# Mamba2 SSD and SwiGLU feed-forward on one core: the order of the steps from the 291st on, and two sums moved from GpSimd to VectorE

## The chip, the cores and the metric

One core of one Trainium2 chip runs the whole kernel in one launch. The metric is the device time of an execution in microseconds (us). The engines are TensorE (PE in the profile; its weight loads are PEld), VectorE (DVE), ScalarE (ACT), GpSimd (POOL) and SyncE (SP), which here issues nearly all the DMAs. Each engine runs its own list of instructions in order, and waits on semaphores for what the others give it.

## The reference

A state-space recurrence over 4 batches and 8 heads is followed by an RMS norm and a SwiGLU feed-forward. In the core of it (shapes: x is 4 x 8 x 768 x 32, B and C are 4 x 8 x 768 x 16, the chunk c is 32 long):

```python
L = np.exp(cum[:, :, :, None] - cum[:, :, None, :]) * causal
CB = np.einsum('bhin,bhjn->bhij', Cc, Bc)
y_intra = np.einsum('bhij,bhjd->bhid', CB * L, xc)
y_inter = np.einsum('bhin,bhnd->bhid', Cc, state) * np.exp(cum)[:, :, :, None]
y[:, :, sl] = y_intra + y_inter
state = decay_full * state + np.einsum('bhjn,bhjd->bhnd', Bc, xc * decay_from_j)
...
x = y.transpose(0, 2, 1, 3).reshape(3072, 256)
xn = x / np.sqrt(np.mean(x * x, axis=-1, keepdims=True) + 1e-06) * rms_g
g = xn @ w_gate                       # 256 -> 1536
out = (g / (1 + np.exp(-g)) * (xn @ w_val)) @ w_out      # 1536 -> 256
```

The weights come in float64, of which the kernel makes float32 itself; the rest is float32, and so is the output of 3072 x 256.

## The kernel before

The 3072 tokens go in six blocks of 512 (numbered 0 to 5). For each block the recurrence is computed in chunks of 128 rows for two pairs of batches, and then the feed-forward; the recurrence of one block runs between the feed-forward products of the one before it, so that TensorE always has something to do.

The products of gate and val of a block are made with seven products in place of eight on 2 x 2 pieces of the operands (steps `P.k.j`, product k of 1 to 7 for column group j of 0 to 5, line 977). They are gathered in two PSUM tiles, named gate and val in the profile; ScalarE copies one (`take`, name `p`, L983), VectorE adds the other (`C.c.j`, name `c`, L989), ScalarE applies silu (L208), and VectorE or GpSimd multiplies (`hid` or `hidp`, L1002), which gives the hidden activations `hid`.

The output projection is made with 20 products (`O.k`, each in two halves h from block 1 on, L1108) whose left factors are hidden pieces or sums of them and whose right factors are pieces of w_out or sums of those. The 16 sums of left factors are listed in `SUMS`; the step `u.n` makes sum n on VectorE and `up.n` makes it on GpSimd (both L1076). Number 7 is a42 = a42 + a43 and number 12 is a21 = a21 - a23, each over 128 x 4 x 128 elements, in place. The right factors (`two` and `twop`, name `two`, L1054) are summed once. The products' totals (`w.n`) are added into the tile `ob` by VectorE (L1139) or copied by ScalarE (L1135), and `put` sends it out (L1144).

In the recurrence, `T` and `g` (L599) make the transposed operands and the products C·B on TensorE, `L` and `L1` (L632) multiply them with the decays on VectorE, reading the PSUM banks of g; `A` (L678), `S` (L686 and L688) carry the states; `y` (L734) is the product that gives the outputs, into the banks that g leaves. `sq` squares y, `ms` (L846) sums the squares on TensorE, `rs` takes the roots on ScalarE and `rb` sends them through DRAM (`roots<-r` L859, then `sq<-roots` L864) so that all partitions have them; `xn` (L873) is the normed input, of which `tx` and `txp` (L954) make the sums that the seven products need. `spread` (DMA, `L<-rowd`, L500), `sub` and `ex` prepare the decays of a later block: an exponential on ScalarE, and a masking of the result on GpSimd (L493). ScalarE has one function table for exponentials and logarithms and one for silu; a step that needs the other one changes it first (L200, L202).

The weights come in 18 pieces. `fetch.k` issues the load of piece k (L184, name `wr`, six buffers), `pow.k` makes its exponents in two passes on ScalarE (name `e`), `man.k` its mantissas on VectorE (name `m`, L224), and `wt.k` joins them (L230). Pieces 12 to 17 are w_out.

What sets the order of all of it is one text of 1725 steps in the kernel, `order`. A step is written block:kind.numbers (with a slash and a number where a place in PSUM is named). The loop below it takes the steps one after the other and issues their instructions, so that the instructions of each engine stand in the order of the text. Some kinds serve the next block or the one after it, whichever block stands in front of the colon.

```python
for step in order.split():
    step, _, slots = step.partition("/")
    blk, _, step = step.partition(":")
    ...
    kind, *numbers = step.split(".")
    ...
        kinds[kind](int(blk), *numbers)
```

Of the kernel before, what the change touches and what calls it, by code (L numbers as in the profile page):

```python
# [20 lines left out]
def kernel(  # L21
# [35 lines left out]
    P = 128  # L57
# [6 lines left out]
    T = NB * S  # L64
# [1212 lines left out]
    def of_chunk(n, fn):  # L1277
# [57 lines left out]
        0:cwp.5.2 1:S.0 1:S.1 0:take.1.5 0:C.11.5 0:P.3.4 0:sq.3 0:man.12 0:cw.0.2 0:P.6.5 0:P.5.5  # L1335
        0:yt.3 0:silug.11.5 0:wt.12 0:hidgp.12.3 3:bc.0 0:C.12.4 0:sq2.2.1.3 0:sq2.2.0.0 0:fetch.17
        0:ms.1 0:take.6.5 0:P.7.5 0:sq2.2.1.2 0:sub.11 0:hidg.21.4 0:silug.22.4 0:hidgp.22.4
        0:sq2.2.0.3 0:sq2.2.1.1 0:fetch.14 0:rs.1 0:rb.1 0:cw.0.1 0:hidg.11.5 0:man.13 0:cwp.5.3
        0:ydone.2 0:man.15 0:take.7.5 0:C.22.5 0:pow.13 0:wt.13 0:o.0/2 0:o.1 0:P.4.5 0:silug.22.5
# [6 lines left out]
        1:silu.11.0 1:P.6.1 0:ex.11 1:P.5.0 0:O.0 0:hidg.12.5 1:two.8 0:O.17 1:P.2.1 0:O.6 0:tx.1.2
        1:two.11 0:cw.1.2 1:two.9 1:take.6.1 1:P.7.1 1:take.7.1 1:P.7.0 0:tx.1.3 1:C.11.1 0:w.5
        0:w.6 1:P.5.1 0:sq2.2.0.1 1:x.1 1:bc.0 0:spread.8 0:u.9 1:T.0.1 1:two.5 1:twop.7 0:O.3 0:w.4
        0:w.10 0:w.1 0:hidgp.22.5 0:up.4 0:u.5 0:up.6 0:cwp.1.3 0:ydone.3 1:silu.11.1 1:take.7.0
        0:hidg.12.4 1:P.4.1 1:silu.21.1 1:hid.21.1 1:cw.2.1 1:C.22.0 1:P.4.0 0:u.7 0:up.8 0:O.9  # L1350
        0:u.10 0:O.18 0:w.8 0:w.12 1:C.22.1 0:w.7 1:hid.11.0 1:P.1.2 0:O.8 0:ex.9 1:P.3.0 1:C.12.0
        0:O.13 1:T.1.1 1:silu.21.0 0:w.11 1:hid.21.0 1:take.1.2 1:Tt.0.1 1:Tt.1.0 1:P.3.1 1:P.6.2
        1:P.2.2 1:two.10 0:u.11 0:u.12 1:hid.11.1 1:twop.4 0:O.7 1:take.6.2 1:P.7.2 0:w.13 0:w.20
        1:C.11.2 0:O.12 0:u.14 0:sq2.2.0.2 0:w.9 1:T.1.0 1:P.1.3 0:O.11 0:w.22 1:sub.3 0:up.13
        0:O.14 0:u.15 0:w.18 1:silu.22.0 1:take.7.2 1:P.4.2 0:O.19 1:silu.12.0 1:hid.12.0
        1:hidp.22.0 1:take.1.3 1:P.6.3 1:ex.3 1:C.12.1 0:w.15 0:w.24 0:O.1 0:O.10 0:w.14 0:w.16
        1:T.0.0 0:w.19 0:w.21 0:w.23 0:w.25 0:put.2 1:sq2.1.0 0:put.0 1:P.2.3 1:P.5.2 1:C.22.2
        1:dT.1 1:spread.1 1:sq2.1.2 1:twop.6 1:cwp.2.3 0:O.5 0:w.17 1:silu.21.2 1:hid.21.2
        1:silu.12.1 1:hidp.12.1 1:take.6.3 1:P.7.3 1:sq2.0.3 0:put.3 1:Tt.0.0 1:silu.22.1
        1:hidp.22.1 1:silu.11.2 1:Tt.1.1 1:g 1:silu.22.2 1:hidp.22.2 1:take.7.3 1:P.4.3 1:silu.21.3  # L1360
        1:C.11.3 0:sub.10 1:silu.11.3 0:sub.8 0:ex.8 1:scale2.0 1:hid.21.3 1:P.3.2 1:C.12.2 1:sub.0
        1:hid.11.3 1:Td.1 1:P.1.4 1:take.1.4 0:ex.10 1:P.5.3 1:C.22.3 1:P.2.4 1:silu.12.2
        1:hidp.12.2 1:P.6.4 1:take.6.4 1:Td.0 1:C.11.4 1:hid.11.2 1:L 1:P.3.3 1:C.12.3 1:P.1.5
        1:take.1.5 2:dT.1 0:put.1 2:dT.0 1:sq2.0.2 1:P.7.4 1:take.7.4 1:P.5.4 1:C.22.4 1:silu.12.3
        1:P.6.5 1:P.2.5 1:L1.2 1:hid.12.3 1:C.11.5 1:P.4.4 1:silu.22.3 1:silu.22.4 1:hidp.22.4
        1:take.6.5 1:silu.21.4 1:silu.11.4 1:hid.21.4 1:hid.22.3 1:silu.11.5 1:hid.11.4 1:hid.11.5
        1:subp.1 1:u.0 1:P.7.5 1:P.5.5 1:take.7.5 1:C.22.5 1:O.15.0 1:P.4.5 1:silu.21.5 1:hid.21.5
        1:up.3 1:u.1 1:O.2.0 1:O.2.1 1:w.0 1:P.3.5 1:L1.3 1:C.12.5 1:O.15.1 1:O.3.0 1:O.3.1
        1:silu.12.5 1:silu.22.5 1:u.2 1:hid.12.5 1:O.0.0 1:O.0.1 1:u.9 1:O.4.0 1:w.2 1:sq2.1.3
        2:bc.0 1:bc.1 1:sq2.1.1 1:w.4 1:w.10 1:y 1:yt 2:T.1.1 2:T.0.1 2:Tt.0.1 1:sq2.0.1 1:sq2.0.0  # L1370
        2:T.0.0 1:scale2.1 2:T.1.0 1:O.16.0 1:O.16.1 1:O.9.0 1:O.9.1 1:w.13 1:u.10 1:P.3.4 1:C.12.4
        1:O.4.1 1:silu.12.4 1:hid.12.4 1:hid.22.5 2:Tt.0.0 2:Tt.1.0 1:up.4 1:up.5 1:O.6.0 1:O.6.1
        1:up.6 1:u.7 1:O.8.0 1:up.11 1:O.8.1 1:O.17.0 1:O.11.0 1:O.17.1 1:O.11.1 1:x.0 2:A 2:sq2.0.0
        2:sq2.1.0 1:sq 1:ms 2:Tt.1.1 2:g 1:w.1 1:w.3 1:w.5 1:w.6 1:rs 1:rb 1:u.8 1:w.18 1:O.18.0
        1:O.13.0 1:O.18.1 1:O.7.0 2:S.0 2:S.1 1:O.7.1 1:O.13.1 1:w.7 1:w.14 1:w.20 1:up.12 1:O.12.0
# [144 lines left out]
```

## Time and profile before

| what | us |
|---|---|
| runs | 388.79, 392.53, 392.95 |
| median of them | 392.53 |
| the profiled execution | 389.72 |
| its span (first to last instruction) | 387.6 |

The span is 2.1 us shorter than the execution's own time; what lies around it is the same for every kernel here. All sums are made against the 389.72. The engine that carries the time is read from the page's busy times and from the chain of work that ended last; where it stands still is read from its timeline, in which a bracket at the end of a row names how long it idled before and what ended that. The first 64 us of the span are set by the loads and the start of the recurrence; 3.2 us at the end pass from the last products to the last output's landing.

### The profile page before, as it was taken

What the parts mean: (1) busy time and instruction counts of PE and PEld (TensorE: products, weight loads), DVE (VectorE), ACT (ScalarE), POOL (GpSimd) and SP (SyncE); (2) the same over time, 40 slices, a digit from 0 to 9 for tenths busy, and PEclk for the clock granted to TensorE, in tenths of its full rate; (3) what the DMA queues carried; (4) which work ended last, traced back from release to release, by engine and by line L of the source; (5) the groups of instructions that cost most, each with busy time, mean ns of one, the idle gap of its engine ahead of it and who ended that gap; (6) DMA issues with size and microseconds to landing.
All of it is one profiled execution on the core that took longest, in us unless ns stands there. A gap on an engine that the chain in (4) does not pass through costs nothing.

```text
span 387.6 us, 9698 instructions
## 1 busy us (share of the span) xinstructions
PE 379.9 (98%) x3837; PEld 329.0 (85%) x3837; DVE 287.2 (74%) x630; ACT 219.9 (57%) x455; POOL 156.6 (40%) x173
## 2 busy tenths in 40 slices
PE   8999999989999999999999999999999999999997
PEld 5675488878988999888998988889988899888996
DVE  7895879979998969666689475787754586545685
ACT  3777778956778371768674374552564641555410
POOL 5021145517754663543587422263721045212141
PEclk9999999999999999999999999999999999999999
DMA  8978997592016333536315240000100001100001
GB/s 92 259 135 225 294 193 149 121 188 41 0 46 124 38 44 72 103 68 109 76 31 84 42 108 2 1 10 27 57 2 3 0 2 35 56 0 2 0 2 54
DMA packets 110084, 28.04 MB, mean 72 GB/s; under 512 B 94840, under 2 KB 107992, under 8 KB 110040
## 3 DMA queue, kind: packets, MB, share of 16 engines
q1 hardware_dynamic: 107960, 27.30, 34.0%
q8 instruction: 30, 0.49, 0.5%
q10 hardware_dynamic: 2080, 0.13, 0.4%
q14 instruction: 14, 0.11, 0.1%
HBM read 23.68 MB, written 3.74 MB: 71 GB/s over the span
## 4 chain that ended last, share of the span: by engine, by line
PE 86%; ACT 4%; DMA 3%; POOL 3%; DVE 2%; issue 1%; DVEq 0%; ACTq 0%; SPq 0%; POOLq 0%
PE gate L977 29%; PE o L1108 22%; PE val L977 21%; PE y L734 3%; PE gate L891 3%; DMA wr<-in_moe_w_out_dram 1%; PE g L599 1%; DMA rowe<-e_sb 1%; ACT e L208 1%; PE gate L901 1%; DMA dT<-rowe 1%; PE e L460 1%; PE g L592 1%; POOL L L493 1%; POOL hid L1076 1%
## 5 line engine op out<-in xcount | busy, mean ns | idle before, releaser
L989 DVE TENSOR_TENSOR c<-val,p 128x512 f32<-128x512 f32 x99 | 67.6, 685 | 36.4 <-PE val L977 29.0
L983 ACT COPY p<-gate 128x512 f32<-128x512 f32 x99 | 56.9, 580 | 44.3 <-PE gate L977 42.6
L977 PE MATMUL gate<-tx,wgv 128*128 128x256 f32 x264 | 66.0, 381 | 0.0
L208 ACT ACTIVATE c<-c 128x256 f32<-128x256 f32 x99 | 39.8, 415 | 40.5 <-DVE c L989 40.1
L977 PEld LDWEIGHTS gate<-tx,wgv 128*128 128x128 f32 x264 | 49.3, 190 | 7.1 <-ACT p L983 0.3
L1002 POOL TENSOR_TENSOR hid<-c 128x256 f32<-128x256 f32 x31 | 24.8, 810 | 65.7 <-ACT c L208 64.7
L1108 PE MATMUL o<-two,hid 128*128 128x128 f32 x308 | 42.7, 276 | 1.7 <-DVE two L1054 0.8
L1139 DVE TENSOR_TENSOR ob<-ob,o 128x128 f32<-128x128 f32 (+1 forms) x116 | 30.8, 293 | 15.6 <-PE o L1108 11.6
L1108 PEld LDWEIGHTS o<-two,hid 128*128 128x128 f32 x308 | 39.3, 192 | 3.4 <-PE o L1108 1.0
L1002 DVE TENSOR_TENSOR hid<-c 128x256 f32<-128x256 f32 x68 | 31.8, 478 | 12.5 <-ACT c L208 12.5
L977 PE MATMUL val<-xn,sw 128*128 128x256 f32 x132 | 34.0, 381 | 0.4 <-DVE c L989 0.4
L977 PE MATMUL val<-tx,sw 128*128 128x256 f32 x132 | 34.0, 380 | 0.0
L977 PE MATMUL val<-xn,wgv 128*128 128x256 f32 x132 | 33.6, 381 | 0.0
L977 PE MATMUL gate<-tx,sw 128*128 128x256 f32 x132 | 33.3, 379 | 0.0
L977 PE MATMUL gate<-xn,wgv 128*128 128x256 f32 x132 | 33.0, 380 | 0.0
L1076 POOL TENSOR_TENSOR s<-s,hid 128x512 f32<-128x512 f32 (+1 forms) x14 | 17.8, 1269 | 28.6 <-PE o L1108 23.7
L1076 POOL TENSOR_TENSOR s<-hid 128x512 f32<-128x512 f32 (+1 forms) x15 | 19.1, 1276 | 22.0 <-DVE hid L1002 18.4
L977 PEld LDWEIGHTS val<-tx,sw 128*128 128x128 f32 x132 | 24.8, 190 | 3.4 <-issue 0.2
L977 PEld LDWEIGHTS val<-xn,wgv 128*128 128x128 f32 x132 | 24.8, 190 | 3.5 <-issue 0.2
L977 PEld LDWEIGHTS gate<-tx,sw 128*128 128x128 f32 x132 | 24.6, 190 | 3.4 <-ACT p L983 0.2
L493 POOL TENSOR_SCALAR_AFFINE_SELECT L<-L 64x512 f32<-64x512 f32 x32 | 22.8, 712 | 11.4 <-ACT L L208 10.1
L977 PEld LDWEIGHTS val<-xn,sw 128*128 128x128 f32 x132 | 24.1, 190 | 3.4 <-DVE c L989 0.5
(211 smaller groups left out, 720.7 us busy)
## 6 DMA issues: line engine op xcount, KB each, us to landing
L<-rowd SPq DMA_DIRECT2D x32, 128.0 KB, 3.2
xr<-in_x_dram SPq DMA_DIRECT2D x24, 128.0 KB, 3.7
wr<-in_moe_w_out_dram SPq DMA_DIRECT2D x6, 511.5 KB
out_dram<-ob SPq DMA_DIRECT2D x23, 128.0 KB, 1.8
wr<-in_moe_w_gate_dram SPq DMA_DIRECT2D x5, 511.5 KB, 4.8
wr<-in_moe_w_val_dram SPq DMA_DIRECT2D x5, 511.5 KB, 5.9
br<-in_B_dram SPq DMA_DIRECT2D x23, 64.0 KB, 3.6
dT<-rowe SPq DMA_DIRECT2D x10, 128.0 KB
```

The costliest lines, as they stand in the source:

```text
L208: nc.scalar.activation(**operands)
L460: nc.tensor.matmul(out=e[:, i], lhsT=ident16, rhs=(whole16 if p < 2 else never16).unsqueeze(1).to_broadcast(m), start=True, stop=False, sk ...
L493: nc.gpsimd.affine_select(out=L[r], in_=L[r], pattern=[[0, L.shape[1]], [1, HC]], compare_op=ALU.is_ge, fill=0.0, base=0, channel_multipli ...
L734: nc.tensor.matmul(out=y[2 * k + u][rows, (2 * n + i) * HC:(2 * n + i + 1) * HC], start=(k, u, rows.start) not in opened, stop=True, skip_ ...
L891: nc.tensor.matmul(out=gv[:, k], lhsT=w[:, t, fs], rhs=xns[0][:, t], start=(t == 0), stop=(t == 1))
L977: nc.tensor.matmul(out=dst[:, half[w]], lhsT=lhsT, rhs=rhs, start=(k in (1, 2, 5) and w == 0), stop=True, skip_group_check=True)
L983: nc.scalar.copy(out=t, in_=Xs[j])
L989: nc.vector.tensor_tensor(out=t, in0=Zs[j], in1=a, op=ALU.add)
L1002: engine.tensor_tensor(out=hid[:, 2 * j + c // 10 - 1, c % 10 - 1], in0=u, in1=src[:, half[1]], op=ALU.mult)
L1076: engine.tensor_tensor(out=hidden_or_sum(o)[:, g], in0=hidden_or_sum(in0)[:, g], in1=hidden_or_sum(in1)[:, g], op=ALU.add if in1[0] == "+" ...
L1108: nc.tensor.matmul(out=Os[blk, b][:, place * P:(place + 1) * P], lhsT=hidden_or_sum(u)[:, g], rhs=rhs, start=(blk, b) not in opened, stop= ...
L1139: nc.vector.tensor_tensor(out=o, in0=o, in1=src, op=ALU.add if what[0] == "+" else ALU.subtract)
```

## The change

The text `order` is another from its 291st entry on: the first 290 steps are the same, and the other 1435 are the same steps in another sequence, but for two: `2:up.7` has become `2:u.7`, and `2:up.12` has become `2:u.12`. So in the third block (number 2) the sums 7 and 12 are made on VectorE and not on GpSimd. All other instructions are the same, in number and form, on each engine. Most steps on TensorE move by four places or fewer; on the queue of SyncE and on ScalarE, VectorE and GpSimd some move further. Where the first two pieces of the text part, and around the two sums:

```diff
-        0:cwp.5.2 1:S.0 1:S.1 0:take.1.5 0:C.11.5 0:P.3.4 0:sq.3 0:man.12 0:cw.0.2 0:P.6.5 0:P.5.5
...
-        3:spread.1 3:sq2.1.2 3:sq2.1.1 2:silu.12.4 2:hidp.12.4 2:up.7 3:g 3:S.0 2:O.9.0 2:O.9.1
...
+        2:O.16.0 2:O.18.0 2:O.16.1 2:O.8.1 2:O.18.1 2:w.16 2:O.5.0 2:hidp.12.4 2:O.5.1 2:u.7
...
+        3:L1.2 3:L1.3 3:y 2:w.12 2:w.17 2:w.13 2:u.12 2:tx.2 2:txp.0 2:tx.1 2:up.8 2:O.12.0 2:O.12.1
```

Three places of it matter for what follows. In the loading of the weights, `0:fetch.16` (the last piece of w_out that is asked for) stood behind `1:spread.0` and now stands ahead of it, and `0:pow.17`, which stood ahead of `0:pow.16`, now follows it:

```diff
-        1:P.1.0 1:P.1.1 1:P.2.0 1:spread.0 0:fetch.16 0:man.16 0:cw.1.1 0:pow.17 0:pow.16 1:spread.2
```

Around the two sums, the steps of the fourth block's recurrence (`3:S`, `3:L`, `3:L1`, `3:y`) stand otherwise among the products of the third block. In the third place, behind the output products O.15 and O.2 of a block, nothing but neighbouring steps has moved. The instructions of the engines at the first two places are shown with the prediction.

More of the change, by code (lines that the diff above doesn't have):

```diff
@@ L1334 @@
         0:hidg.21.3 0:spread.10 0:spread.9 0:P.1.5 0:spread.11 0:silug.12.3 0:C.22.4 0:P.2.5
-        0:cwp.5.2 1:S.0 1:S.1 0:take.1.5 0:C.11.5 0:P.3.4 0:sq.3 0:man.12 0:cw.0.2 0:P.6.5 0:P.5.5
[L1336 to L1339, printed above, removed]
@@ L1346 @@
[L1346 to L1351, printed above, removed]
@@ L1352 @@
[L1352 to L1374, printed above, removed]
```

245 lines of the change are left out of this document (139 added, 106 removed).

## The prediction

> **What bounds the kernel now.** I read the profile in this order: the page's busy times, the chain that ended last, the view by stretches, then the timeline of TensorE where it stands still. First two lines of the page: the busy time of each engine, and the chain of work that ended last, split by engine.
>
> ```profile
> PE 379.9 (98%) x3837; PEld 329.0 (85%) x3837; DVE 287.2 (74%) x630; ACT 219.9 (57%) x455; POOL 156.6 (40%) x173
> PE 86%; ACT 4%; DMA 3%; POOL 3%; DVE 2%; issue 1%; DVEq 0%; ACTq 0%; SPq 0%; POOLq 0%
> ```
>
> TensorE carries the time; everything else can only make it wait. The change leaves TensorE's instructions as they are, so what it can win is TensorE's standing time behind the first moved step. The view by stretches gives that (the numbers behind an engine are its busy us and its count, then the granted clock, the DMA share and GB/s).
>
> ```profile
> 64.00:90.00 26.00, 24.81 (x127) 21.27 (x126) 22.63 (x47) 19.43 (x39) 11.49 (x11) 1.00 0.78 151
> 90.00:200.00 110.00, 109.99 (x1292) 98.26 (x1291) 88.65 (x199) 71.87 (x145) 60.68 (x63) 1.00 0.35 61
> 200.00:256.00 56.00, 55.14 (x497) 50.01 (x496) 40.49 (x81) 29.21 (x64) 25.08 (x24) 1.00 0.22 45
> 256.00:384.40 128.40, 128.24 (x1115) 117.78 (x1115) 82.46 (x175) 54.61 (x129) 40.66 (x43) 1.00 0.05 17
> ```
>
> The clock is 1.00 throughout. TensorE idles 1.19 us in the first row, .86 in the third, and .01 and .16 in the other two: from 90 to 200 and from 256 on there is nothing to win, only something to lose. The rows before 64 us and behind 384.4 hold the same steps in the same order in both kernels.
>
> Busy time hides part of a wait, since a waiting group's first matmul is drawn longer. So I go by the spacing of matmuls where nothing waits: 12.70/112 = .113 us for a 128x128 record of the output projection, and 1.73/8 = .216 for a 128x256 record of gate and val (from the chain, with starts in us, then duration).
>
> ```profile
> 258.88 12.70 PE o L1108 x112
> 291.93 1.73 PE gate L977 x8
> ```
>
> TensorE's timeline at its three stops:
>
> ```profile
> 84.30 0.79 PE L1108 MATMUL o<-wo,hid 128*128 128x128 f32 x4
> 85.90 0.68 PE L1108 MATMUL o<-two,hid 128*128 128x128 f32 x4 [0.81 <-DVE two L1054]
> 86.97 0.71 PE L1108 MATMUL o<-two,hid 128*128 128x128 f32 x4 [0.39 <-POOL two L1054]
> 87.51 0.61 PE L1108 MATMUL o<-wo,hid 128*128 128x128 f32 x4
> ```
>
> ```profile
> 207.24 1.03 PE L977 MATMUL gate<-xn,wgv 128*128 128x256 f32 x4
> 208.77 1.16 PE L1108 MATMUL o<-two,hid 128*128 128x128 f32 x8 [0.50 <-POOL hid L1076]
> ```
>
> ```profile
> 251.20 1.50 PE L1108 MATMUL o<-two,hid 128*128 128x128 f32 x12
> 253.06 1.13 PE L977 MATMUL val<-xn,sw 128*128 128x256 f32 x4 [0.36 <-DVE c L989]
> ```
>
> From 84.30 to 87.51 stand 12 records, 12 x .113 = 1.36, so 3.21 - 1.36 = 1.85 us are lost. At 208.77: 207.24 + 4 x .216 = 208.10, lost .67. At 253.06: 251.20 + 12 x .113 = 252.56, lost .50. Together 3.02: if all of it went and nothing came, the profiled execution would end at 389.72 - 3.02 = 386.7. That is 2.81 below the median of the runs (392.53), which is as much as the whole prize; 1% of the median (3.9 us) is about what a measurement of this kernel can tell from no change.
>
> **First edit: the loads of the last w_out piece (64 to 90 us).** SyncE's queue, and the chain's transfer that it starts:
>
> ```profile
> 70.52 0.41 SPq L859 DMA_DIRECT2D roots<-r  x1
> 73.84 1.75 SPq L864 DMA_DIRECT2D sq<-roots  x4
> 75.69 1.09 SPq L500 DMA_DIRECT2D L<-rowd  x2
> 76.88 0.52 SPq L184 DMA_DIRECT2D wr<-in_moe_w_out_dram  x1
> ```
>
> ```profile
> 76.88 5.32 DMA wr<-in_moe_w_out_dram
> 82.28 0.79 ACT L208 ACTIVATE e<-wr,kinks 128x512 f32<-128x512 int16 x1 [3.49 <-DMA wr<-in_moe_w_out_dram]
> ...
> 83.10 0.72 ACT L208 ACTIVATE e<-e,kinks 128x512 int32<-128x512 f32 x1
> ...
> 83.86 1.29 DVE L230 TENSOR_TENSOR wo<-m,e 128x512 int32<-128x512 int32 x2 [0.54 <-ACT e L208]
> 85.07 0.68 DVE L1054 TENSOR_TENSOR two<-wo 128x512 f32<-128x512 f32 x1
> ```
>
> The piece is asked for at 76.88, lands 5.32 later, is turned from float64 into float32 by two ACT passes and one DVE pass, summed once, and only then TensorE goes on at 85.90. In SyncE's order before, the last piece stands behind two masks' rows (`L<-rowd`); `wr` is the raw piece, `roots` the norms on their way out and `sq` on their way back:
>
> ```order
> L184 DMA wr<-in_moe_w_out_dram 128x2x1023
> L859 DMA roots_1188<-r_1184 128x128
> L864 DMA sq<-roots_1188 32x4x128 x4
> L500 DMA L<-rowd 64x512 x2
> L184 DMA wr<-in_moe_w_out_dram 128x2x1023
> ```
>
> And in the changed kernel, with what now stands ahead of it:
>
> ```order
> L150 DMA xr<-in_x_dram 128x8x32 x2
> L133 DMA squares<-in_B_dram 32x16x16 x2
> L143 DMA br<-in_B_dram 128x8x16 x2
> L184 DMA wr<-in_moe_w_out_dram 128x2x1023 x2
> L859 DMA roots_1176<-r_1172 128x128
> L864 DMA sq<-roots_1176 32x4x128 x4
> L184 DMA wr<-in_moe_w_out_dram 128x2x1023
> L133 DMA squares<-in_C_dram 32x16x16 x6
> L500 DMA L<-rowd 64x512 x4
> ```
>
> The two rows of `L<-rowd` have moved behind the piece, as have the loads of squares; an `xr` load has come to the front. Without the two rows the piece is issued 76.88 - 75.69 = 1.19 us sooner. The sums that the norms wait for (ms.1) stand one product step earlier on TensorE, 4 x .216 = .86, and with them the roots: 1.19 + .86 = 2.05 sooner, issue at 74.83, landing at 80.15. Against it, the exponents of piece 17 now follow those of 16 on ACT instead of preceding them, and the factor needs the later: 80.15 + .79 + .72 = 81.66, another 1.51 for piece 17 = 83.17, DVE's last half of 1.29 = 83.8, its sum .68 = 84.5. TensorE reaches that factor at 84.30 + 4 x .113 = 84.75. So the stop at 85.90 goes, barely, and of the smaller ones behind it, which wait for GpSimd's sums of the same pieces, I leave .35: gain 1.85 - .35 = 1.5. Bounds: the whole 1.85, or nothing, if the `xr` load put ahead (it waits for its buffer) or the roots' round trip eat the 2.05. Below nothing: piece 17 late by its whole 1.51. I take 1.5 because 2.05 stands against a need of 1.15 (85.90 - 84.75). The `L<-rowd` rows that move back are read a block later by ACT, which idles in this stretch (19.43 busy of 26.00); losing that cover costs nothing before TensorE's next use of the masks. The other permutations in this stretch are steps of the same work moved by some places: 0.
>
> **Second edit: the boundary of the third and fourth block (198 to 212 us).** On GpSimd `hid<-hid` 128x4x128 are the two sums in question, the first of them followed by `s<-s,hid`, and L493 is the masking of the decays; before:
>
> ```order
> L493 AFFINE_SELECT L<-L 64x512 x2
> L1002 TENSOR_TENSOR hid<-c 128x256
> L1076 TENSOR_TENSOR hid<-hid 128x4x128
> L1076 TENSOR_TENSOR s<-s,hid 128x512
> L493 AFFINE_SELECT L<-L 64x512 x4
> L1076 TENSOR_TENSOR hid<-hid 128x4x128
> L954 TENSOR_TENSOR tx<-xn 128x256
> ```
>
> After, on GpSimd:
>
> ```order
> L493 AFFINE_SELECT L<-L 64x512 x4
> L1002 TENSOR_TENSOR hid<-c 128x256
> L493 AFFINE_SELECT L<-L 64x512 x2
> L1076 TENSOR_TENSOR s<-s,hid 128x512
> L954 TENSOR_TENSOR tx<-xn 128x256
> ```
>
> And on VectorE after (before, the two `hid<-hid` rows were not there and `xn` stood ahead of all `L`):
>
> ```order
> L688 SCALAR_TENSOR_TENSOR S<-S,fcol,A 128x64 x3
> L1139 TENSOR_TENSOR ob<-ob,o 128x128
> L1076 TENSOR_TENSOR hid<-hid 128x4x128
> L632 TENSOR_TENSOR L<-g,L 128x2x4x128
> L873 SCALAR_TENSOR_TENSOR xn<-yt,gcol,sq 128x512 x2
> L632 TENSOR_TENSOR L<-g_2657,L 128x4x128
> L632 TENSOR_TENSOR L<-g_2658,L 128x4x128
> L1139 TENSOR_TENSOR ob<-ob,o 128x128 x2
> L1076 TENSOR_TENSOR hid<-hid 128x4x128
> ```
>
> The sums have left GpSimd, where the second stood behind four masks; the first now stands on VectorE ahead of all that the next block's y needs. Rows of the two engines there:
>
> ```profile
> 198.12 2.08 DVE L688 SCALAR_TENSOR_TENSOR S<-S,fcol,A 128x64 f32<-128x64 f32 x3
> 200.12 0.68 DVE L1076 TENSOR_TENSOR s<-hid,s 128x512 f32<-128x512 f32 x1
> ...
> 202.82 2.53 DVE L688 SCALAR_TENSOR_TENSOR S<-S,fcol,A 128x64 f32<-128x64 f32 x3
> ...
> 207.51 2.40 DVE L632 TENSOR_TENSOR L<-g,L 128x1024 f32<-128x1024 f32 x3
> L688 DVE SCALAR_TENSOR_TENSOR S<-S,fcol,A x36: 273/285/1382, 18.0 to 273.6; 128x64 f32<-128x64 f32 x36
> ```
>
> ```profile
> 200.31 1.07 POOL L1002 TENSOR_TENSOR hid<-c 128x256 f32<-128x256 f32 x1 [0.18 <-ACT c L208]
> 201.46 1.28 POOL L1076 TENSOR_TENSOR hid<-hid 128x512 f32<-128x512 f32 x1
> 202.69 1.27 POOL L1076 TENSOR_TENSOR s<-s,hid 128x512 f32<-128x512 f32 x1
> 203.91 3.14 POOL L493 TENSOR_SCALAR_AFFINE_SELECT L<-L 64x512 f32<-64x512 f32 x4
> 207.14 1.58 POOL L1076 TENSOR_TENSOR hid<-hid 128x512 f32<-128x512 f32 x1
> ```
>
> The stop of .67 at 208.77 waits for the second sum (207.14 + 1.58 = 208.72). In the changed order y comes ahead of the product that reads it, so this stop goes: -.67. But y now follows the gate product directly and is due at 208.10, and it needs VectorE's last `L`, which before ended at 207.51 + 2.40 = 209.91, just as y began. The first sum stands in front: + .68, by the row of a sum on VectorE; 210.59. Some comes back: the six `S` rows above took 4.61 us where six of the shortest would be 6 x .273 = 1.64; they lost 2.97 beside GpSimd's run of work from 198.12 to 205.35. Of these 7.23 us the first sum was 1.28, so a share of .53 returns, and VectorE's wait of .39 for TensorE before 201.19 may go as well: 210.59 - .53 - .39 = 209.67. TensorE waits 209.67 - 208.10 = 1.57 at y, and the edit costs 1.57 - .67 = +.9. Bounds: -.67 if VectorE is in time after all; 210.59 - 208.10 - .67 = +1.8 if nothing comes back. I take +.7, a little under the sum, since `xn` now stands between the `L`, and TensorE's gate product waits for it too, so that part of the two waits is one.
>
> The Trainium skill, page "SBUF — State Buffer", section "Who interferes with whom", says that a DVE instruction with two SBUF inputs contends with a GpSimd instruction that reads SBUF, and that the shared pair of ports is an exclusive lock held for a whole instruction. The trace agrees as far as it goes: the shortest `S` is 273 ns and the longest 1382, about one whole GpSimd sum longer. By that rule each GpSimd sum removed would return up to its full duration to VectorE, which is the first rival below.
>
> **Third place, 253.06.** The product that waits for `c` stands behind the same steps in both orders: 0; bounds -.50 and, if the chain from the gate's silu is pushed by a row such as .68, +.68. The rest, from 90 to 198 and from 212 on, is order within stretches with .17 us of idle time: 0, up to +1 (one and a half stops of .67).
>
> Sum: 389.72 - 1.5 + .7 = 388.9.
>
> **Rivals.** *VectorE in time at y.* The two sums took 1.28 + 1.58 = 2.86 us of GpSimd's time and take 2 x .68 = 1.36 of VectorE's. If VectorE gets the difference of 1.5 back in its `S`, `xn` and `L` rows, y's wait of 1.57 is gone: 389.72 - 1.5 - .67 = 387.5. For it: the `S` rows' spread of 273 to 1382. Against: the four masks stay, and only the first sum lies ahead of `L`.
>
> *The weights come no sooner*, held up by the `xr` load or the roots: 389.72 + .7 = 390.4; with the runs' own scatter upward, up to 392.5. For it: the queue is one, in order, and SyncE's `sq<-roots` waits 73.84 - 70.93 = 2.9 us, which no order of loads shortens.
>
> *Slower: the first sum is held on VectorE.* It needs `hid<-c`, which GpSimd now does behind two more masks, 3.14/2 = 1.57, and those masks wait for an exponential ahead of which ACT now changes its function table to silu and back; a change takes 1.28:
>
> ```profile
> 198.45 1.28 ACT L200 ACT_TABLE_LOAD   x1
> ```
>
> If both delays add in full, `hid<-c` starts at 200.31 + 1.57 + 2 x 1.28 = 204.44 and ends at 205.51. VectorE is ready for the sum at 205.35 - .53 - .39 = 204.43: the rival decides from there, and everything behind the sum (`L`, `xn`, and so y and the gate product) is late by the excess, 1.08: 388.9 + 1.1 = 390.0. With a third change of table in the way, 391.3, which is slower than the profiled execution by 1.6. For it: ACT changes its table some times between 194 and 207 us. Against: some of the two delays overlap, and GpSimd has one sum less ahead.
>
> **How the numbers follow.** Forecast .42: 388.9, by itself 388.1 to 390.0. VectorE in time .20: 387.5. Weights no sooner .23: 390.4 to 392.5. Sum held .15: 390.0 to 391.3, and more with the weights late too. The runs lay from .93 below the profiled execution to 3.23 above it, so each case has a tail upward; hence 392.7 as the upper end, with .12 above, and 387.0 below, with .07 under it. Faster by over 1% is below 388.6: the second case almost whole and a third of the first, .18 + .14 = .32. Slower by over 1% is above 396.4: .04, from the last case and the tails. Within 1%: .64.
>
> **What would show it.** Right: the first factor's row at about 84.8 with no wait for `two`; the last `wr` asked for at about 75; no wait for GpSimd's `hid` near 208, and instead a wait of 1 to 2 us for VectorE's `L` ahead of y; all other stretches with as little idle as before. Wrong: a wait for `two` of .8 still there, y begun without one, or a new stop of over 1 us between 90 and 198 or behind 256.

## The result

The changed kernel took 387.08 us as the median of 9 runs (385.85 to 387.81), the kernel before 392.16 (9 runs, 388.79 to 393.12): a ratio of 0.9892, 95% interval 0.9858 to 0.9927. The forecast was 388.9 with a range of 387.0 to 392.7. The profiled execution of the changed kernel took 387.79 us with a span of 386.0, against 389.72 and 387.6 before. So the two profiled executions differ by 1.93 us, and the medians by 5.1; the runs of before lie 4.3 us apart, those of the changed kernel 2.0. The scatter is therefore a large part of this result. Runs more than 1.5% above the fastest run of the same kernel are left out of the ratios here and below, and three of 649, 784 and 1367 us out of every count. A ratio is worked out from all the other runs and is not the quotient of the two medians.

Two stretches of the changed kernel, in the view of the prediction (behind the stretch and its length: busy us of TensorE, of its weight loads, VectorE, ScalarE, GpSimd, each with a count; the granted clock, the DMA share, GB/s):

```profile
64.00:90.00 26.00, 26.00 (x135) 22.68 (x135) 24.87 (x53) 20.37 (x40) 11.52 (x12) 1.00 0.69 152
200.00:256.00 56.00, 55.36 (x587) 49.65 (x592) 38.08 (x82) 26.39 (x63) 22.51 (x22) 1.00 0.20 41
```

TensorE's idle time from 64 to 90 us, 1.19 before, is gone, and from 200 to 256 .64 is left of .86. TensorE's timeline where the stops were, now in the weights' stage and at the boundary of the blocks:

```profile
85.14 0.61 PE L1108 MATMUL o<-wo,hid 128*128 128x128 f32 x4
85.59 0.61 PE L1108 MATMUL o<-two,hid 128*128 128x128 f32 x4
86.03 0.61 PE L1108 MATMUL o<-wo,s 128*128 128x128 f32 x4
86.48 1.03 PE L977 MATMUL gate<-tx,sw 128*128 128x256 f32 x4
```

```profile
203.06 2.05 PE L1108 MATMUL o<-two,hid 128*128 128x128 f32 x16
205.53 1.16 PE L1108 MATMUL o<-two,s 128*128 128x128 f32 x8 [0.42 <-POOL s L1076]
206.53 1.03 PE L977 MATMUL gate<-xn,wgv 128*128 128x256 f32 x4
207.49 0.34 PE L734 MATMUL y<-T,S 32*64 32x64 f32 x8
208.05 0.77 PE L734 MATMUL y<-T,S 32*64 32x64 f32 x48 [0.22 <-DVE L L632]
208.75 1.51 PE L734 MATMUL y<-L,xr 64*32 64x64 f32 x128
```

The same products of y in the profile before:

```profile
209.86 0.90 PE L734 MATMUL y<-T,S 32*64 32x64 f32 x56
210.69 1.48 PE L734 MATMUL y<-L,xr 64*32 64x64 f32 x128
```

The four rows of the first piece follow each other at .45 us, which is four records at .112: no stop at all. In the second piece 16 records from 203.06 on would end at 204.86, and the next product begins at 205.53: .67 us are lost to sum 11 on GpSimd. The first products of y, 8 and 48 records, take 1.26 us (207.49 to 208.75), where the 56 took .83 before: .43 us are lost there to VectorE's `L`, of which the bracket names .22. At the third place (253 before) no row shows a wait any more. Stops of 3.02 us have become .67 + .43 = 1.10, which is 1.92 us less.

How much shorter TensorE's work became in all can be read at two products that stand at the same place among its instructions in both kernels: the y product of step 0:y.3, among the first 290 steps, and the last product of all. Before, and then in the changed kernel:

```profile
61.16 0.46 PE L734 MATMUL y<-T,S 32*64 32x64 f32 x24
...
384.08 0.69 PE L1108 MATMUL o<-wo,s 128*128 128x128 f32 x4
```

```profile
62.00 0.46 PE L734 MATMUL y<-T,S 32*64 32x64 f32 x24
...
382.49 0.69 PE L1108 MATMUL o<-wo,s 128*128 128x128 f32 x4
```

From the one to the other pass 322.92 us before and 320.49 in the changed kernel: 2.43 less, and 2.41 less in a second profile of the changed kernel (60.39 to 380.90). This is called TensorE's stretch below. The stops are 1.92 of the 2.43. The other .5 lies in gaps of .1 to .2 us between products, for which no row names a reason: by the same spacing, the profile before has 11 of them between 62 and 130 us, 1.18 us in all, and this one 5, with .51.

The two executions differ by less than 2.43, because this one reached the y product of 0:y.3 .84 us later, in work that both kernels have in common. And .33 us came off outside the span, which is 2.12 us shorter than the execution before and 1.79 in the changed kernel: 2.43 - .84 + .33 = 1.92. So what lies around the span is not the same for every kernel. In the runs listed below it is 2.0 to 2.2 us in each run of before and 1.7 to 1.8 in each of the changed kernel; no run shows what sets it.

The last piece of w_out, on SyncE's queue and on ScalarE:

```profile
74.33 1.74 SPq L864 DMA_DIRECT2D sq<-roots  x4
76.25 0.39 SPq L184 DMA_DIRECT2D wr<-in_moe_w_out_dram  x1
76.68 3.43 SPq L133 DMA_DIRECT2D squares<-in_C_dram  x6
80.15 2.41 SPq L500 DMA_DIRECT2D L<-rowd  x4
```

```profile
80.10 0.79 ACT L208 ACTIVATE e<-wr,kinks 128x512 f32<-128x512 int16 x1 [2.03 <-DMA wr<-in_moe_w_out_dram]
...
81.55 0.76 ACT L208 ACTIVATE e<-wr,kinks 128x512 f32<-128x512 int16 x1
```

It was asked for at 76.25, only .63 earlier than before (1.47, if the .84 of the later start are taken off), but it landed 3.85 us after that and not 5.32 (read at the start of the ScalarE pass that waited for it).

### The profile page after: what moved, and what is told of

It is laid out like the page before. It is cut to its first block, busy times and chain, and to the rows that moved or that the text cites. A ratio compares the mean times of both kernels' runs of the same rounds, so it can differ in the third digit from the quotient of the medians.

```text
span 386.0 us, 9707 instructions
## 1 busy us (share of the span) xinstructions
PE 379.9 (98%) x3837; PEld 330.1 (85%) x3837; DVE 282.1 (73%) x632; ACT 219.7 (57%) x455; POOL 152.3 (39%) x171
## 4 chain that ended last, share of the span: by engine, by line
PE 92%; DMA 3%; DVE 1%; SPq 1%; ACT 1%; issue 1%; DVEq 0%
PE gate L977 30%; PE o L1108 23%; PE val L977 22%; PE y L734 3%; PE gate L891 3%; PE o L1009 3%; PE g L599 1%; DMA rowe<-e_sb 1%; PE gate L901 1%; DMA dT<-rowe 1%; PE e L460 1%; PE g L592 1%; DMA L<-rowd 1%; SPq L143 0%; PE idle L328 0%
## 5 line engine op out<-in xcount | busy, mean ns | idle before, releaser
L208 ACT ACTIVATE c<-c 128x256 f32<-128x256 f32 x99 | 39.0, 414 | 25.4 <-DVE c L989 25.1
L1002 DVE TENSOR_TENSOR hid<-c 128x256 f32<-128x256 f32 x68 | 30.1, 455 | 7.9 <-ACT c L208 7.5
L493 POOL TENSOR_SCALAR_AFFINE_SELECT L<-L 64x512 f32<-64x512 f32 x32 | 22.0, 686 | 14.8 <-ACT L L208 13.7
L1002 DVE TENSOR_TENSOR hid<-u,gate 128x256 f32<-128x256 f32 x33 | 13.6, 417 | 18.5 <-ACT u L208 18.5
```

Of the source, the lines that this page charges most:

```text
L208: nc.scalar.activation(**operands)
L493: nc.gpsimd.affine_select(out=L[r], in_=L[r], pattern=[[0, L.shape[1]], [1, HC]], compare_op=ALU.is_ge, fill=0.0, base=0, channel_multipli ...
L1002: engine.tensor_tensor(out=hid[:, 2 * j + c // 10 - 1, c % 10 - 1], in0=u, in1=src[:, half[1]], op=ALU.mult)
```

## The experiments

The kernels were measured in three sets (the rows with the same time of before are one), each on another chip and with the kernel before beside them. The median of before went from 388.8 to 390.2 from set to set (392.16 in the first measurement), so ratios are compared within a set, and the microseconds below are differences of medians against the before of that set.

| kernel | median us | before us | ratio, 95% interval |
|---|---|---|---|
| w_after | 387.87 | 390.16 | 0.9946 (0.9922 to 0.9969) |
| w_before | 388.74 | 390.16 | 0.9946 (0.9917 to 0.9976) |
| fetch_first | 387.92 | 390.16 | 0.9945 (0.9917 to 0.9973) |
| third_place | 390.31 | 390.16 | 1.0006 (0.9969 to 1.0042) |
| changed_again | 386.21 | 389.16 | 0.9904 (0.9870 to 0.9937) |
| sums_back | 388.36 | 389.16 | 0.9970 (0.9947 to 0.9992) |
| sums_only | 392.38 | 389.16 | 1.0060 (1.0030 to 1.0091) |
| one_wait_less | 388.05 | 389.16 | 0.9972 (0.9941 to 1.0002) |
| late_roots_before | 391.91 | 388.82 | 1.0064 (1.0030 to 1.0098) |
| late_roots_changed | 386.08 | 388.82 | 0.9948 (0.9926 to 0.9970) |
| two_steps | 387.00 | 388.82 | 0.9958 (0.9942 to 0.9973) |
| sum_eleven | 386.78 | 388.82 | 0.9950 (0.9933 to 0.9968) |

One thing bears on all of these rows. Each run has a mean granted clock of TensorE; in most it is .999 or 1.000, called full clock here, and in some .996 or lower. Among the runs of before these are 16 of 35 in the first set, 5 of 27 in the second and 1 of 23 in the third. In the first set they took 390.80 to 393.99 us with a median of 391.3; the other 19 took 387.75 to 390.70 with a median of 389.14. Of the kernels that ask early for the last piece of w_out (w_after, fetch_first, changed_again, sums_back, late_roots_changed, two_steps and sum_eleven) 1 run of 67 has the lower clock, of the other five 13 of 58. The one such run with a trace is the profiled one of sum_eleven, with a mean of .995. Its clock is 1.00 but for these two stretches, and TensorE's rows there are:

```profile
36.00:40.00 4.00, 2.64 (x24) 1.44 (x25) 3.09 (x7) 1.16 (x2) 0.00 (x0) 0.86 1.02 266
40.00:44.00 4.00, 4.00 (x8) 1.57 (x7) 3.22 (x7) 3.48 (x6) 0.00 (x0) 0.72 1.04 269
```

```profile
37.36 0.65 PE L599 MATMUL g<-T 32*64 32x128 f32 x20 [1.48 <-DVE T L573]
37.94 8.83 PE L891 MATMUL gate<-xn,wgv 128*128 128x512 f32 x16
```

The same in the profile of the changed kernel, at a clock of 1.00:

```profile
38.06 7.13 PE L891 MATMUL gate<-xn,wgv 128*128 128x512 f32 x16
```

The 16 products take 8.83 us in place of 7.13: 1.70 are lost, right behind a wait of 1.48 for VectorE (.74 in the changed kernel). This lies ahead of the 291st step. No profile shows where the runs of before lose their clock.

**w_after and w_before: the order cut in two at the 417th step.** One has the changed order ahead of the cut and that of before behind it, the other the reverse.

```diff
-        0:cwp.5.2 1:S.0 1:S.1 0:take.1.5 0:C.11.5 0:P.3.4 0:sq.3 0:man.12 0:cw.0.2 0:P.6.5 0:P.5.5
...
-        1:P.1.0 1:P.1.1 1:P.2.0 1:spread.0 0:fetch.16 0:man.16 0:cw.1.1 0:pow.17 0:pow.16 1:spread.2
...
```

> The first 417 steps (to about 88 us, all of the weights' loading) in the changed order, all behind them in the order of before, no sum moved. Theory S (the runs of before differ among themselves because the last piece of w_out lands late by varying amounts, and in the old order each microsecond of it is lost): no wait for two left in the profile, the runs' spread falls from about 4 us to about 2, median 388.3, that is 4 us faster than before (ratio .990). Theory T (the scatter comes from elsewhere and stays; only the 1.85 us of the profiled stop go): median 1.9 us faster (ratio .995), spread as before.

> The complement: the first 417 steps in the order of before, the rest as changed, both sums on VectorE. Theory S: the stop for two at 85 us stays, the spread of the runs stays about 4 us, median 1.0 us faster than before (the stops at 208 and 253, .67 and .52, less the .58 of the new one: ratio .998). Theory T: the gain of the rest is 392.2 - 387.1 - 1.9 = 3.2 us (ratio .992).

w_after was 2.3 us faster, and 11 of its 12 runs lie between 387.49 and 388.34, where those of before went from 387.75 to 393.99. Its profile is of the twelfth, which took 1367 us, and says nothing of the others. w_before was 1.4 us faster and its runs lie between 387.57 and 389.95. By the spread, theory S holds for the first half, since the scatter goes with the weights' stage, and not for the second, whose spread should have stayed at 4 us. By the ratios S is missed twice (.990 and .998 lie outside the intervals). T's ratios of .995 and .992 lie inside, the second barely, but its 3.2 us for the second half came out as 1.4. Part of both gains is the clock of before: against its 19 runs at full clock the medians are 1.3 and .4 us lower.

In w_before's profile TensorE's stretch is .54 us shorter than before. Its stop for the two factors at 85 us, where its order is that of before, happens to be .58 smaller (1.19 in place of 1.77, counted at these two products alone). So the second half, without the first, leaves TensorE's stretch about as it was; what it brings is some .35 us outside the span (1.67 to 1.77 in all its runs). The two halves' 1.3 and .4 us at full clock do not add up to the 2.76 that the whole order gives below, on another chip: what each brings is not separated.

**fetch_first: one load moved.** The smallest form of the first edit.

```diff
-        0:sq2.2.0.3 0:sq2.2.1.1 0:fetch.14 0:rs.1 0:rb.1 0:cw.0.1 0:hidg.11.5 0:man.13 0:cwp.5.3
+        0:sq2.2.0.3 0:sq2.2.1.1 0:fetch.14 0:rs.1 0:rb.1 0:fetch.16 0:cw.0.1 0:hidg.11.5 0:man.13 0:cwp.5.3
...
-        1:P.1.0 1:P.1.1 1:P.2.0 1:spread.0 0:fetch.16 0:man.16 0:cw.1.1 0:pow.17 0:pow.16 1:spread.2
+        1:P.1.0 1:P.1.1 1:P.2.0 1:spread.0 0:man.16 0:cw.1.1 0:pow.17 0:pow.16 1:spread.2
```

> Before, with one DMA moved: the last piece of w_out is asked for straight behind the roots' return, ahead of the two rows of L<-rowd. If the place in the queue is what made it late, it is issued 1.2 us sooner, and TensorE's stop at 85 us falls from 1.85 to .7 at most; if it also lands in about 3.9 us in place of 5.3, since the rows of L<-rowd are no longer in flight ahead of it, the stop goes. Median 1.2 to 1.9 us faster (ratio .995 to .997). Rival: the landing is bound by the bytes in flight, whatever the order: the landing time grows by what the issue gains, ratio 1.000.

It was 2.2 us faster, as much as the whole order ahead of the cut, and its 12 runs lie between 387.48 and 388.95, all at full clock. Against the runs of before at full clock it is 1.2 us faster, and TensorE's stretch is .99 shorter. SyncE's queue in its profile, and the ScalarE pass that reads the piece:

```profile
73.43 1.74 SPq L864 DMA_DIRECT2D sq<-roots  x4
75.27 0.39 SPq L184 DMA_DIRECT2D wr<-in_moe_w_out_dram  x1
75.76 2.37 SPq L500 DMA_DIRECT2D L<-rowd  x4
```

```profile
79.19 0.78 ACT L208 ACTIVATE e<-wr,kinks 128x512 f32<-128x512 int16 x1 [0.88 <-DVE wo L230]
```

The load follows the roots at once, and at 79.19 ScalarE no longer waits for it but for a buffer that VectorE frees: the piece had landed by 3.9 us after its issue. The rival, that the landing is bound by the bytes in flight whatever their order, is out. TensorE's stop for the first factor is gone, and .46 us are left at the next, which GpSimd makes. What the old place costs differs from one execution to the next: the stop for the first factor is 1.15 us in the profile before, 1.08 in one_wait_less, .76 in late_roots_before, .58 in w_before, .34 in sums_only and .04 in third_place. In the seven profiles with the load ahead it is nil.

**third_place and one_wait_less: why the stop at 253 went.** In the profile before, VectorE's sum 3 took 1.79 us there, where the same form takes .69, and GpSimd's first sum had begun .03 us ahead of it. The first try moved a multiplication between:

```diff
-        3:C.22.5 4:Td.0 3:P.4.5 3:silu.21.5 3:hid.21.5 3:P.4.2 3:silu.21.2 3:hid.21.2 3:u.3 3:P.5.2
+        3:C.22.5 4:Td.0 3:P.4.5 3:silu.21.5 3:P.4.2 3:silu.21.2 3:hid.21.2 3:hid.21.5 3:u.3 3:P.5.2
```

> Before, with one step moved: in the fourth block hid.21.5 stands behind hid.21.2 on VectorE in place of ahead of it, as in the changed order. Theory: at 250.6 us VectorE's sum u.3 took 1.79 us because a sum of GpSimd began .03 us ahead of it; with another multiplication between the releasing one and u.3, VectorE begins first, u.3 takes .69 and the stop of .52 us at 253 goes (-.5 us, ratio .9987). Rival: GpSimd's sum gets in first all the same, since it is released by the same multiplication, u.3 takes 1.8 and the stop stays or grows by the .4 us of the moved step.

It missed. The two engines' rows in its profile, GpSimd's first:

```profile
249.35 1.27 POOL L1076 TENSOR_TENSOR s<-hid 128x512 f32<-128x512 f32 x1 [6.30 <-DVE hid L1002]
```

```profile
249.37 1.79 DVE L1076 TENSOR_TENSOR hid<-hid 128x512 f32<-128x512 f32 x1
```

GpSimd began .02 us ahead, sum 3 took 1.79 again and the stop was .85. What still told the two kernels apart is what sum 3 waits for: in the kernel before it waits on a counter of VectorE's and on one of GpSimd's, since an earlier sum of GpSimd (number 0) reads the piece that sum 3 overwrites. The profile before has a separate wait of VectorE's at this line, just ahead of sum 3:

```profile
L1076 DVEq EVENT_SEMAPHORE  x1: 21/21/21, 250.6 to 250.6; - x1
```

The changed kernel has none there. So the next kernel makes sum 0 on VectorE:

```diff
-        3:P.3.4 3:C.12.4 3:P.2.2 3:hid.12.3 3:hid.11.3 3:up.0 4:T.1.0 3:silu.12.4 3:P.6.5 3:take.6.5
+        3:P.3.4 3:C.12.4 3:P.2.2 3:hid.12.3 3:hid.11.3 3:u.0 4:T.1.0 3:silu.12.4 3:P.6.5 3:take.6.5
```

> Before, with sum 0 of the fourth block on VectorE in place of GpSimd, at the same place in the text. Sum 3, which took 1.79 us near 250.6, then waits on VectorE's own work alone and no longer on GpSimd's counter as well, as in the changed kernel. Theory: the second wait costs some .06 us, by which GpSimd's sum got in first; now VectorE begins first, sum 3 takes .7 us, GpSimd's takes 1.8, and TensorE's stop of .52 us at 253 goes: .5 us faster (ratio .9987). Rival: GpSimd still begins first and nothing changes there.

```profile
250.83 0.69 DVE L1076 TENSOR_TENSOR hid<-hid 128x512 f32<-128x512 f32 x1
```

```profile
250.88 1.78 POOL L1076 TENSOR_TENSOR s<-hid 128x512 f32<-128x512 f32 x1 [12.55 <-DVE hid L1002]
```

Now VectorE is first by .05 us, takes .69, GpSimd pays, the separate wait is gone, and so is TensorE's stop at 253. GpSimd's sum begins .08 to .09 us after the multiplication ahead of it ends, in every profile of this place; VectorE's begins .10 to .11 after it with the separate wait (before, third_place, fetch_first) and .03 to .04 without (one_wait_less, w_before, the changed kernel). The median fell by 1.1 us, with an interval that reaches from -2.3 to +.1; the .5 us lie in it but are not measured by it. The rows show the mechanism, and TensorE's stretch is .54 us shorter.

**changed_again, sums_back and sums_only: what the two sums are worth.**

> The changed kernel once more, beside the other runs of this call. If the share of each part is the same on any chip, its median is 3 us under before (the 2.2 us that one moved DMA gave, and .5 to 1 us more), its runs within 2 us of each other, and its profile shows the same single stop of about .6 us near 205 us. If the gain of the first measurement came from its chip, it shrinks to 2 us.

The changed kernel was 2.95 us faster than before here, with 6 runs within .9 us, and 2.76 faster than the runs of before at full clock. TensorE's stretch is 2.41 shorter and .33 us less lie outside the span, which makes 2.74 in all.

```diff
-        2:O.16.0 2:O.18.0 2:O.16.1 2:O.8.1 2:O.18.1 2:w.16 2:O.5.0 2:hidp.12.4 2:O.5.1 2:u.7
+        2:O.16.0 2:O.18.0 2:O.16.1 2:O.8.1 2:O.18.1 2:w.16 2:O.5.0 2:hidp.12.4 2:O.5.1 2:up.7
...
-        3:L1.2 3:L1.3 3:y 2:w.12 2:w.17 2:w.13 2:u.12 2:tx.2 2:txp.0 2:tx.1 2:up.8 2:O.12.0 2:O.12.1
+        3:L1.2 3:L1.3 3:y 2:w.12 2:w.17 2:w.13 2:up.12 2:tx.2 2:txp.0 2:tx.1 2:up.8 2:O.12.0 2:O.12.1
```

> The changed order with both sums of the third block back on GpSimd (2:up.7, 2:up.12). Theory that the sums' engine matters here: sum 7 then lengthens GpSimd's queue ahead of the masks and of sum 11, for which TensorE waits .58 us near 205: sum 11 comes 1.28 us later and the stop grows to 1.8; VectorE gets .68 back, which does not help as it waited for the masks anyway: 1.2 us slower than the changed kernel. Rival: the sums' engine is worth nothing beside the order: within .3 us of the changed kernel.

With both sums back on GpSimd and the changed order kept, 2.15 us of that were lost, more than the 1.2 expected. TensorE in its profile, then VectorE's `xn` and the two engines' rows beside it:

```profile
204.82 1.16 PE L1108 MATMUL o<-two,s 128*128 128x128 f32 x8 [1.28 <-POOL s L1076]
205.81 1.03 PE L977 MATMUL gate<-xn,wgv 128*128 128x256 f32 x4
207.75 0.34 PE L734 MATMUL y<-T,S 32*64 32x64 f32 x8 [0.91 <-DVE L L632]
```

```profile
204.59 2.41 DVE L873 SCALAR_TENSOR_TENSOR xn<-yt,gcol,sq 128x512 f32<-128x512 f32 x2
203.50 1.26 POOL L1076 TENSOR_TENSOR s<-s,hid 128x512 f32<-128x512 f32 x1
204.84 1.62 POOL L1076 TENSOR_TENSOR hid<-hid 128x512 f32<-128x512 f32 x1
```

The stop for sum 11 grew from .67 to 1.54, less than the 1.8 expected, and y begins 1.0 us later behind the gate product than in the changed kernel, which was not expected. The masks for `L` come .9 later on GpSimd, as sum 11 does. Then `xn`, which stands between the `L`, takes 2.41 us beside GpSimd's two sums, where it takes 1.40 in the changed kernel. So the sums' engine is worth something twice, in GpSimd's order and in the time of VectorE's own instructions. TensorE's stretch is 1.87 longer than in the changed kernel.

```diff
-        3:spread.1 3:sq2.1.2 3:sq2.1.1 2:silu.12.4 2:hidp.12.4 2:up.7 3:g 3:S.0 2:O.9.0 2:O.9.1
+        3:spread.1 3:sq2.1.2 3:sq2.1.1 2:silu.12.4 2:hidp.12.4 2:u.7 3:g 3:S.0 2:O.9.0 2:O.9.1
...
-        2:up.12 2:O.12.0 2:O.12.1 2:w.13 2:w.22 2:tx.2 3:y 2:txp.0 2:tx.1 2:tx.3 2:w.17 2:w.8 2:up.8
+        2:u.12 2:O.12.0 2:O.12.1 2:w.13 2:w.22 2:tx.2 3:y 2:txp.0 2:tx.1 2:tx.3 2:w.17 2:w.8 2:up.8
```

> Before with nothing changed but the two sums, on VectorE. Theory of the record: VectorE is the engine that is late at y there; .67 us of TensorE's wait at 208.8 go with the second sum, and about as much comes as a wait for the first sum or at y: between -.67 and +1.4 us, ratio .998 to 1.003. Rival: the sums alone bring what the whole boundary brings, the stop at 208.8 is gone and no other comes: -.67 (ratio .9983).

The sums alone, in the order of before, made it 3.2 us slower, beyond both theories. VectorE's rows of the two sums, and TensorE:

```profile
199.07 0.69 DVE L1076 TENSOR_TENSOR hid<-hid 128x512 f32<-128x512 f32 x1 [3.19 <-POOL hid L1002]
...
209.10 0.67 DVE L1076 TENSOR_TENSOR hid<-hid 128x512 f32<-128x512 f32 x1
```

```profile
207.25 1.03 PE L977 MATMUL gate<-xn,wgv 128*128 128x256 f32 x4
209.82 1.16 PE L1108 MATMUL o<-two,hid 128*128 128x128 f32 x8 [1.55 <-DVE hid L1076]
```

Where the first sum now stands, VectorE waits 3.19 us for GpSimd's multiplication and holds all that stands behind it; by the spacing of its matmuls TensorE stops 1.90 us at 201.8. The second sum stands behind VectorE's `L` and ends late, and TensorE waits 1.7 for it where it waited .67. So the engine and the place belong together: the change of engine without the order costs 3.2 us, the order without the change of engine gives only 0.8.

**late_roots_before and late_roots_changed: how much lateness each order bears.** In the profile of third_place there was a loss that its edit does not explain: VectorE's `xn` of the fifth block waited 1.88 us for the norms' return, and TensorE, behind sums and totals of VectorE, lost .91 and 1.22 us by the spacing.

```profile
265.83 1.41 DVE L873 SCALAR_TENSOR_TENSOR xn<-yt,gcol,sq 128x512 f32<-128x512 f32 x2 [1.88 <-DMA sq<-roots]
```

```profile
267.50 0.71 PE L1108 MATMUL o<-sw,hid 128*128 128x128 f32 x4 [0.74 <-DVE ob L1139]
269.17 1.60 PE L1108 MATMUL o<-sw,hid 128*128 128x128 f32 x12 [0.96 <-DVE ob L1139]
```

To give both kernels such a late return, it was sent twice for that block:

```diff
-        for k in range(P // 32):
+        for k in (range(P // 32) if blk != 4 else 2 * list(range(P // 32))):
             nc.sync.dma_start(
```

> Before, with the return of the fifth block's norms (sq<-roots, near 260 us) sent twice, the second time over the same place, so that it is whole about 2 us later; nothing is left out. Theory: part of the scatter of before is this round trip through DRAM, since in one profile it came 1.9 us late and TensorE lost 2.0 us behind VectorE's xn. Then the dose of about 2 us costs 1.7 to 2.2 us in the profile's stops between 262 and 275 us. Rival: there is slack, under .5 us.

> The changed kernel with the same doubled return. Theory that the changed order tolerates late loads: xn stands behind two more output products' worth of VectorE's work and one sum (u.14) has gone ahead of it; the 2 us cost under 1.0 us. Rival: the order is no more tolerant here than before: 1.7 to 2.2 us, as in the run beside it.

VectorE's rows in the order of before, and then in the changed order:

```profile
266.12 1.42 DVE L873 SCALAR_TENSOR_TENSOR xn<-yt,gcol,sq 128x512 f32<-128x512 f32 x2 [1.64 <-DMA sq<-roots]
267.45 0.28 DVE L1139 TENSOR_TENSOR ob<-ob,o 128x128 f32<-128x128 f32 x1
267.65 1.56 DVE L1076 TENSOR_TENSOR hid<-hid 128x512 f32<-128x512 f32 x1
```

```profile
263.40 1.42 DVE L873 SCALAR_TENSOR_TENSOR xn<-yt,gcol,sq 128x512 f32<-128x512 f32 x2 [0.39 <-DMA sq<-roots]
264.73 1.24 DVE L1139 TENSOR_TENSOR ob<-ob,o 128x128 f32<-128x128 f32 x5
```

In the order of before `xn` waits 1.64 us with a sum of left factors behind it, and TensorE stops twice, .67 and 1.22 us, within what was expected; the median is 3.1 us over before, 2.0 when only runs at full clock are compared. In the changed order the norms' return is waited for .39, the sum has already been made, and TensorE loses .17; the median, 386.08, is that of the changed kernel without the dose (386.21, in the set before). The changed order bears a late return that costs the other 1.9 us in the profile.

**two_steps and sum_eleven.** The first joins the two small edits that had paid, fetch_first's and one_wait_less's.

> Before with two steps changed: the last piece of w_out asked for straight behind the roots' return, and sum 0 of the fourth block on VectorE. If these two carry most of what the changed kernel gains, and the boundary of the third and fourth block nearly nothing, it is 2.2 + .5 = 2.7 us faster than before (ratio .993), against 3.0 for the changed kernel. Rival: the order of the rest carries it: 2.2 us or less.

It was 1.8 us faster than before, in runs from 386.64 to 387.39: less than the 2.7 expected, and by its number the rival's case. Against 386.08 and 386.21, the medians of the changed kernel with the dose and without, .8 to .9 us are left to the rest of the order. In its profile no stop for the first factor and none at 253 is left; .46 at the second factor and .70 at the boundary are. The changed kernel has saved the first and has 1.10 at the boundary, so by the stops the two would be about equal. TensorE's stretch is .58 us longer in two_steps all the same: its gaps of .1 to .2 us between 62 and 130 us are 13 with 1.47 us, where the changed kernel has 5 with .51. Another .1 us lies outside the span. What opens or closes these gaps is not shown.

```diff
-        2:O.13.0 2:O.13.1 2:ex.2 3:L 2:up.11 2:O.11.0
+        2:O.13.0 2:O.13.1 2:ex.2 2:u.11 3:L 2:O.11.0
```

> The changed kernel with one more sum of the third block, number 11, on VectorE, ahead of the next block's L. VectorE idles .55 us there for the masks, and TensorE waits .58 for this sum on GpSimd. Theory: the sum fits in that gap (.68 of .55), the stop near 204 goes and the one at y grows from .22 to about .35: .45 us faster than the changed kernel, that is 3.4 under before. Rival: L starts later by contention with GpSimd's masks and y's stop takes back all of it.

Another sum on VectorE did not pay: 386.78, against 386.08 for late_roots_changed in the same set. The stop of .67 for sum 11 went, but the sum took 1.14 us beside GpSimd's masks and not .68, the gate product that needs `xn` now waits .77, and y begins .40 behind that product in place of .10. TensorE's stretch is the changed kernel's within .1 us (320.57). The rival, that y's stop takes it all back, holds. None of these is shown to be faster than the changed kernel.

## Why the prediction was right

The direction was right, and so was that the weights' stage carries the gain: of the stops 1.85 us went there, and .07 at the other two places together. The measured 387.08 lies inside the range by .08 us, and that is partly luck. In the profiles the changed kernel is worth 2.76 us (2.43 in TensorE's stretch and .33 outside the span); the rest of the 5.1 us between the medians goes with the scatter of before in that measurement, of whose runs no clock is on record. Measured again, the changed kernel had a median of 386.21, beside a before that was 3.0 us lower as well. Point by point:

- *The loads of the last w_out piece, gain 1.5.* All of the 1.85 went. (The sum had nothing for the small gaps between products, of which .67 us less are left between 62 and 130 us.) The issue came 1.47 earlier, with the later start taken off, not 2.05: the norms' return was asked for .35 sooner and not .86. But the prediction carried the 5.32 us of landing over, and that was 3.85: the rows of `L<-rowd` moved behind it were no longer ahead of it in the DMA engines. With the later start taken off, the piece was there at 79.26 and not at 80.15; that the profile has 80.10 is chance. The rival in which the weights come no sooner fell with that.
- *The boundary, cost .7.* The stops were .67 and are 1.10: +.43, but made up otherwise than forecast. The mis-sized term is what VectorE gets back from GpSimd, put at .53 by shares. Rows of VectorE there, in the changed kernel:

```profile
197.26 1.61 DVE L688 SCALAR_TENSOR_TENSOR S<-S,fcol,A 128x64 f32<-128x64 f32 x3
...
200.71 1.68 DVE L688 SCALAR_TENSOR_TENSOR S<-S,fcol,A 128x64 f32<-128x64 f32 x3
...
205.30 1.40 DVE L873 SCALAR_TENSOR_TENSOR xn<-yt,gcol,sq 128x512 f32<-128x512 f32 x2
L688 DVE SCALAR_TENSOR_TENSOR S<-S,fcol,A x36: 275/285/785, 18.8 to 271.0; 128x64 f32<-128x64 f32 x36
```

  The two groups of `S` took .47 and .85 less than before, `xn` .72 less (it was 2.12), 2.04 in all, and the longest `S` fell from 1.382 us to .785. So y waits .43 and not 1.57; the rival "VectorE in time at y", which put the return at 1.5, was nearer. Against that the prediction did not see the new wait of .67 for sum 11, which GpSimd now makes behind two more masks; it costed the masks only for the sum that had moved. That wait stands ahead of y and hides as much of VectorE's work. So one of the signs that it named, a wait of 1 to 2 us at y, did not come.
- *The third place, 0.* It was -.50. "The product that waits for `c` stands behind the same steps in both orders" was so, and the stop went nevertheless, because it hung on which of two engines began .03 us sooner.
- *The rival on the other side* had the right mechanism, a sum on VectorE held by GpSimd's `hid<-c`, and sums_only shows its price: TensorE stops 1.9 us at the first sum, not 1.1, and the kernel loses 3.2 with the second. The changed order avoids it by placing the sum further back: `hid<-c` is done at 202.31 there and the sum begins at 202.92, without a wait.
- *The scatter.* The prediction gave every case the same tail upward, the one of the runs of before. (Its 2.81 us are the distance of the profiled execution from the median, not that of 386.7.) The changed kernel has lost most of the tail: 2.0 us between its runs against 4.3, .9 against 4.7 when measured again. The chance of .32 for faster by over 1% rested on that tail; the two measurements are at 1.1 and 1.0%.

What in the changed order takes scatter out is shown in two places: the load that stands earlier (in fetch_first 1.5 us between its runs and none at a lower clock, and no stop for the first factor) and the late return that no longer stops TensorE (the two late_roots). It stays open whether and how an early load keeps the clock up, since the one loss of clock with a trace lies near 40 us, ahead of all that moved. It also stays open why fetch_first and two_steps have little scatter, though the fifth block's `xn` stands in them as in before: one profile for each kernel does not tell how often that return is late, and no run tried whether the loads near 75 us have a bearing on one near 260.

## What to carry to other kernels

Ask for the load that ends a chain ahead of the loads that nobody needs soon, however small they are: it gains its place in the queue, and here a shorter flight as well. Move work to another engine only together with its place in that engine's order, and look first for what it would wait for there. Where runs scatter, compare the granted clock of each run before you compare medians, and look for the load with no slack, since a single profile shows a mild case as easily as a bad one. And measure between two instructions that both kernels share: that gave 2.43 and 2.41 us where the medians gave 5.1 and 2.95.

## What the runs showed of the hardware

- A load of 512 KB landed 5.2 to 5.4 us after its issue behind two loads of `L<-rowd`, in six profiles (before, 76.88 to 82.2; w_before, 76.18 to 81.39; third_place, 75.42 to 80.70; also late_roots_before, one_wait_less and sums_only), and 3.5 to 4.4 us with those loads behind it, in five (the changed kernel 3.85, changed_again 3.51, sums_back 3.94, late_roots_changed 4.39, sum_eleven 3.95).
- Of a VectorE sum and a GpSimd sum that begin within .05 us of each other, the one that begins first takes its own time (.69 on VectorE, 1.27 on GpSimd) and the other waits (1.79 and 1.78). That is what the Trainium skill, page "SBUF — State Buffer", section "Who interferes with whom", says of issue order; the rows agree. They add that here a second semaphore to wait for was enough to lose: from the end of the multiplication ahead, sum 3 begins about .1 us later with the two, about .03 with the one.
- Two `xn` of 128x512 on VectorE took 1.40 us in the changed kernel at the boundary, and 2.41 in sums_back, where two of GpSimd's sums run beside them.
- A run's mean granted clock of .995 was one loss of 1.7 us (sum_eleven, 37.94 to 46.77 us, clock .86 and .72 in two stretches of 4 us), right behind a wait of TensorE's of 1.48 us. Runs of before at .990 to .996 took 391.3 us in the median of the first set, those at full clock 389.14.
- The time from sending the norms to their return's first issue was 1.6 us for the fifth block in the profiles before and after (259.77 to 261.38 and 257.38 to 259.00) and 3.9 in third_place (258.53 to 262.41), in kernels with the same loads.
